# Attention kernel: the last head in two halves, own matmul orders for four of a head's eight pairs of steps, and the first phase's balances and copies issued at other places

## The chip, the cores and the metric

The kernel runs on one core of a Trainium2 chip. The metric is the device time of one execution in microseconds (us), as the median of several runs.

## The reference

Two attentions of 32 heads (head width 18, sequence 2048, width 576) are computed from the same `x` and mixed by a gate. In attention B all heads share one key and one value.

```python
def _A_ref(x, wqkv, wo):                       # 32 heads, each with its own k and v
    ...
    scores = jnp.einsum("bhqd,bhkd->bhqk", q, k) * scale
    p = _softmax(scores, axis=-1)
    o = jnp.einsum("bhqk,bhkd->bhqd", p, v)
    ...
def _B_ref(x, wq, wk, wv, wo):                 # k = x @ wk, v = x @ wv, shared
    ...
g = _sigmoid((x * gate_w).sum(-1, keepdims=True))
return g * a + (1 - g) * b
```

## The kernel before, in words

**First phase.** `project` multiplies the weights (14 column tiles, split into a high and a low float32r part) with `x` in 56 jobs of 14 matmuls each. `evict` rounds each result to two float16 parts on ScalarE and VectorE and writes them to DRAM. The factors `tv` that the evictions need come from `balance`: VectorE reduces the weights' sizes to `br` (line 201 or 206), TensorE turns it (209), VectorE forms `bd` (211 to 214), TensorE spreads it (219), VectorE makes `tv` (221 to 231). It is a generator; the tuple `at` names the matmuls of a job ahead of which it is continued. `shared_v` turns the shared values on TensorE and copies them to `vb` on VectorE (287), which frees a bank of PSUM.

**Second phase.** 64 heads `u`, 16 steps each; a step is one tile of 128 keys (and, 22 steps ahead, one tile of 128 queries for the maxima). The loop takes two steps at a time, A and B, so a head is eight pairs (T%16 = 0, 2, ... 14). A pair issues what a string lists, in that order, on TensorE:

- `sA0`..`sB3`: scores of 512 queries (line 551) into a bank of `ps` (four banks); ScalarE takes the exponential into `pt` (558).
- `mA0`..`mB3`: 512 scores of a head that comes 22 steps later (514) into a bank of `pm` (three banks); VectorE takes the row maximum into `mx` (523). `x` is a matmul with differences of keys; ScalarE puts its positive part into `xb` (517), and the `mA0` of the next pair is a VectorE operation that adds `xb` and takes the maximum (520, `junk`, followed by a read of its accumulator into `mx`). So `mA1` falls away, and a pair has seven such operations on VectorE and nine on ScalarE.
- `P`, or its halves `p` and `f`: step T-2's values times `pt`, summed in `acc` (564). `Q`, or `h` and `H`: the same for step T-1. A half has 256 columns, a whole one 512.
- `U`: a unit of the output projection (12 matmuls at line 678 and one sum on VectorE, or on ScalarE for heads 33 to 53).

Scores use the upper rows of the array and maxima the lower ones, so a score and a maximum that are neighbours in the string run side by side.

When a head's sum is complete (after `Q` of the pair T%16 = 0), `head_out` copies `acc` to `oe` on VectorE (574), and the next head's first product must wait for that. In the pair T%16 = 10, `max_rows` puts a reduction (529) and a transposition (531) on VectorE ahead of the pair's maxima.

The strings are `PLAIN` for most pairs, `END` for T%16 = 0, `AFTER` for T%16 = 2, and `UNIT`, `UNIT_END`, `UNIT2` where units of the output projection are due: in heads 33 to 53 in the pairs 0 and, every second head, 10; from step 944 on in every pair. From step 1002 there are no maxima left (`ALONE`).

**Tail.** After the last head, `last_out` copies `acc` (709, 710), turns it (713), scales it (717 to 719), turns it back (722), splits it (724, 725), sends it by DMA into `end` beside rows that `normalise(8)` has scaled (lines 602 to 621), and runs 32 units of three matmuls (735) and one sum on VectorE (738); each finished 128 rows of the output go out by DMA. `idle` issues matmuls whose results are not used.

Of the kernel before, what the change touches and what calls it, by code (L numbers as in the profile page):

```python
# [49 lines left out]
def gated_mix_kernel(ctx: ExitStack, tc: tile.TileContext, xT, wall, wv, wo, out):  # L50
# [277 lines left out]
    with tc.tile_pool(name="xs", bufs=6, side="right") as xsp:  # L328
# [215 lines left out]

    def step_scores(u, i, c, alone):
# [5 lines left out]
        nc.tensor.matmul(ps, kst(u)[b:b + 56, i * P:(i + 1) * P],  # L551
                         qs[u % 3][b:b + 56, c * 512:(c + 1) * 512], start=True, stop=True)
        PT["q"] = PT.get("q", []) + [(c, ps)]
        if alone and c == 0:
            return
        for c, ps in PT.pop("q"):
            pt = L["pt"].tile([P, 512], F32, name="pt")
            nc.scalar.activation(pt, ps, AF.Exp, scale=SCALE / LIFT ** 2)  # L558
            PT[u, i, c] = pt

    def step_pv(u, i, a, b):

        for j in range(4):
            nc.tensor.matmul(acc[32 * j:32 * j + 19, a:b], v_of(u, i), PT[u, i, j][:, a:b],  # L564
                             start=(i == 0 and a == 0), stop=(i == 15), skip_group_check=True)
        if b == 512:
            for j in range(4):
                del PT[u, i, j]

    OT = {}  # L570
# [19 lines left out]
    def normalise(t, at_end=False):  # L590
# [9 lines left out]
        yield  # L600
        yield
        nc.vector.reciprocal(sm[:n, :], sm[:n, :])
        (nc.vector if at_end else nc.gpsimd).tensor_tensor(sm[:n, :], sm[:n, :], gt[:n, :], op=OP.mult)
        yield
        dma(r_d[u0:u1, :].rearrange("h (s f) -> (h s) f", f=P), sm[:n, :])
        yield
        ot = OT.pop(t)
        R = L["work"].tile([P, S], F32, name="R", bufs=1)
        r0 = P * t
        while r0 < P * t + rows:  # L610
            u = r0 // DH
            n = min(DH * (u + 1), P * t + rows) - r0
            dma(R[r0 - P * t:r0 - P * t + n, :], r_d[u:u + 1, :].to_broadcast([n, S]))
            r0 += n
        yield
        if at_end:
            L["end"] = {y: L["pool"].tile([P, S], F32R, name=f"end{y}") for y in "hl"}
            for c in range(4):
                cs = slice(512 * c, 512 * c + 512)
                yield  # L620
                nc.vector.tensor_tensor(ot[:rows, cs], ot[:rows, cs], R[:rows, cs], op=OP.mult)
                split(ot[:rows, cs], L["end"]["h"][:rows, cs], L["end"]["l"][:rows, cs], nc.vector, nc.vector)
            return
# [74 lines left out]

    def last_out():

        oe, ot = (L["work"].tile([P, 512], F32, name=x, bufs=1) for x in ("oe", "oT"))
        oh, ol = (L["work"].tile([P, 512], F32R, name=x, bufs=1) for x in ("oh", "ol"))
        end = L["end"]

        def idle(n):
            for _ in range(n):
                nc.tensor.matmul(acc, qs[0][0:54, 0:P], qs[0][0:54, 0:512], start=True, stop=True)

        nc.scalar.activation(oe[:, 0:256], acc[:, 0:256], AF.Copy)
        nc.vector.tensor_copy(oe[:, 256:512], acc[:, 256:512])  # L710
        pt, pb = end_bank(), end_bank()
        for c in range(4):
            nc.tensor.transpose(pt[:, P * c:P * c + P], oe[:, P * c:P * c + P], ident)
        idle(5)
        r = L["work"].tile([P, 16], F32, name="rl")
        p4, o4 = (x.rearrange("p (c j d) -> p c j d", c=4, d=32) for x in (pt, ot))
        nc.vector.reciprocal(r.rearrange("p (j c) -> p c j", c=4), p4[:, :, :, DH])
        nc.vector.tensor_tensor(r, r, L["g"], op=OP.mult)
        nc.vector.tensor_tensor(o4, p4, r.rearrange("p (j c) -> p c j", c=4).unsqueeze(3).to_broadcast([P, 4, 4, 32]),
                                op=OP.mult)  # L720
        for c in range(4):
            nc.tensor.transpose(pb[:, P * c:P * c + P], ot[:, P * c:P * c + P], ident)
        idle(14)
        nc.scalar.activation(oh, pb, AF.Copy)
        nc.vector.tensor_tensor(ol, pb, oh.bitcast(F32), op=OP.subtract)
        r0 = DH * (NU - 1) - 8 * P
        for j in range(4):
            dma(end["h"][r0:P, 512 * j:512 * j + 512], oh[32 * j:32 * j + DH, :])
            dma(end["l"][r0:P, 512 * j:512 * j + 512], ol[32 * j:32 * j + DH, :], nc.scalar)
        w = WO[8]  # L730
        for st_ in range(16):
            for hf in range(2):
                fp = end_bank()
                for n, (a, b) in enumerate(PRODS):
                    nc.tensor.matmul(fp[:, 0:288], end[b][:, st_ * P:(st_ + 1) * P],
                                     w[a][:, 0, 288 * hf:288 * hf + 288], start=(n == 0), stop=(n == 2))
                dst = L["oacc"][:, st_, 288 * hf:288 * hf + 288]
                nc.vector.tensor_tensor(dst, fp[:, 0:288], dst, op=OP.add)  # L738
            dma(out[st_ * P:(st_ + 1) * P, :], L["oacc"][:, st_, :], nc.scalar if st_ % 2 else None)

# [14 lines left out]
    def when(T, f):  # L755
        at.setdefault(T, []).append(f)
# [46 lines left out]
    ALONE = "sA0 sA1 P U sA2 sA3 U sB0 sB1 h U sB2 sB3 H U"  # L803
    LEADS = "mA0 MA1 mA2 MA3 V.A mB0 MB1 mB2 MB3 V.B"
    order = None
    for T in range(-LEAD, NSTEP + 2, 2):
        if T == 0:
# [8 lines left out]
        order = LEADS if T < 0 else FIRST if T == 0 else ALONE if alone else (UNIT2 if T >= SEG[1][3] else UNIT_END if T % 16 == 0 else UNIT) if units else \  # L816
            END if T % 16 == 0 else AFTER if T % 16 == 2 and T > 2 else PLAIN
        for op in order.split():
# [12 lines left out]
            elif k == "s":  # L831
                if T < NSTEP:
                    step_scores(*divmod(T + second, 16), int(c), alone)
            elif k == "U":
                pull(min(units, 1))
                units -= min(units, 1)
            elif T >= 2:
# [13 lines left out]
    pull(10 ** 9)  # L851
    last_out()

# [33 lines left out]
```

## Time and profile before

| | |
|---|---|
| median of 3 runs | 2686.05 us (2685.97 to 2687.71) |
| profiled execution | 2688.33 us, its span 2686.0 us |
| TensorE busy | 2665.6 us (99%), 22697 matmuls |
| VectorE busy | 2428.2 us (90%) |
| ScalarE busy | 2402.0 us (89%) |
| first phase, until the first exponential | 277.2 us |
| second phase, until the last exponential ends | to 2659.0 us |
| tail | 27.0 us |

Rows of the profile give a start in us, a duration, engine, line, operation, `written<-read`, shapes and a count; `[0.17 <-PE pm L514]` says that the engine had been idle for 0.17 us and what ended that. "Busy" counts overlapping instructions once, so an engine that is busy all the time can still be waiting inside its instructions.

### The profile page before, as it was taken

Reading aid. Unit: us, or ns where it says so; the run is one execution under the profiler, and the core shown is the slowest. Engines: PE = TensorE matmul, PEld = TensorE weight load, DVE = VectorE, ACT = ScalarE, POOL = GpSimd, SP = SyncE. Lnnn points to the kernel's source line nnn. Section 1 sums busy time; section 2 is a strip of 40 time slices with the busy share of each in tenths; the row PEclk is TensorE's granted clock in tenths of the full one; section 3 lists DMA queues with packets and bytes.
Section 4 is the critical chain, followed back from the end, with each engine's and each line's share of the span. In section 5 each row is a group of like instructions: output and inputs, shape, how many; then the busy total and the mean of one; then the engine's idle time right before and its main releaser. Section 6 shows DMA issues by size and latency. Waiting matters only on the chain.

```text
span 2686.0 us, 59393 instructions
## 1 busy us (share of the span) xinstructions
PE 2665.6 (99%) x22697; PEld 905.2 (34%) x22697; DVE 2428.2 (90%) x4586; ACT 2402.0 (89%) x4810; POOL 278.8 (10%) x518
## 2 busy tenths in 40 slices
PE   9999999999999999999999999999999999999999
PEld 6778322222222222222222222322222232223444
DVE  7447999999999999999999999999999999998863
ACT  4341899999999999999999999999999999998875
POOL 4740000001001100100110002000200011011000
PEclk9999999999999999999999999999999999999999
DMA  6332000011001100210132112122121212122312
GB/s 201 124 112 78 21 20 20 19 37 40 28 17 46 44 20 18 54 32 20 36 76 82 43 51 85 42 56 58 57 67 50 56 52 61 39 71 85 89 36 94
DMA packets 126904, 150.19 MB, mean 56 GB/s; under 512 B 55272, under 2 KB 94344, under 8 KB 125421
## 3 DMA queue, kind: packets, MB, share of 16 engines
q1 hardware_dynamic: 112175, 119.08, 15.7%
q0 software_dynamic: 7968, 19.23, 2.1%
q10 hardware_dynamic: 6476, 8.08, 0.9%
q8 instruction: 178, 2.92, 0.5%
q14 instruction: 107, 0.88, 0.1%
HBM read 90.80 MB, written 46.45 MB: 51 GB/s over the span
## 4 chain that ended last, share of the span: by engine, by line
PE 84%; DVE 12%; issue 2%; DMA 1%; ACT 1%; SPq 0%; DVEq 0%; POOL 0%; ACTq 0%; POOLq 0%
PE acc L564 35%; PE ps L551 20%; PE pm L514 14%; DVE mx L523 7%; PE pm L678 4%; PE ps L514 3%; PE pm L248 3%; PE ps L248 2%; PE ps L297 2%; DVE junk L520 2%; DVE oe L574 1%; ACT pt L558 0%; SPq L56 0%; DVE oacc L738 0%; DVE norm_a L190 0%
## 5 line engine op out<-in xcount | busy, mean ns | idle before, releaser
L558 ACT ACTIVATE pt<-ps 128x512 f32<-128x512 f32 x4074 | 2109.1, 645 | 64.7 <-PE ps L551 47.0
L523 DVE TENSOR_REDUCE mx<-pm 128x1 f32<-128x512 f32 x3072 | 1918.4, 682 | 70.9 <-PE pm L514 34.5
L551 PE MATMUL ps<-qs,ksb 56*128 56x512 f16 x2688 | 810.5, 380 | 0.0
L514 PE MATMUL pm<-ksb,qs 54*128 54x512 f16 x2341 | 768.2, 381 | 1.9 <-DVE mx L523 0.6
L564 PE MATMUL acc<-pt,vb 128*19 128x512 f32 (+1 forms) x6392 | 598.5, 446 | 1.8
L564 PE MATMUL acc<-pt,vg 128*19 128x256 f32 (+1 forms) x5904 | 585.7, 468 | 1.2 <-DVE oe L574 0.5
L514 PEld LDWEIGHTS <-qs 54*128 54x128 f16 x4096 | 292.1, 94 | 598.0 <-issue 532.5
L551 PE MATMUL ps<-qs,ksa 56*128 56x512 f16 x1386 | 412.1, 380 | 0.7
L514 PE MATMUL pm<-ksa,qs 54*128 54x512 f16 x1232 | 401.4, 380 | 2.2 <-DVE mx L523 1.2
L520 DVE CUSTOM_DVE_ANT_0 junk<-pm,xb 128x512 bf16<-128x512 f32 x501 | 341.5, 682 | 11.1 <-PE pm L514 6.7
L551 PEld LDWEIGHTS <-ksb 56*128 56x128 f16 x2688 | 198.3, 93 | 402.5 <-issue 370.9
L517 ACT ACTIVATE xb<-ps 128x512 f32<-128x512 f32 x501 | 310.5, 620 | 7.7 <-PE ps L551 7.3
L564 PEld LDWEIGHTS acc<-pt,vb 128*19 128x19 f32 x6392 | 108.3, 96 | 248.1 <-issue 232.0
L533 POOL TENSOR_SCALAR mt<-mt 128x32 f32<-128x32 f32 x64 | 18.5, 290 | 1631.5 <-DVE mt L531 1631.5
L564 PEld LDWEIGHTS acc<-pt,vg 128*19 128x19 f32 x5904 | 100.7, 97 | 231.4 <-issue 223.9
L551 PEld LDWEIGHTS <-ksa 56*128 56x128 f16 x1408 | 100.3, 94 | 203.9 <-issue 186.7
L514 PE MATMUL ps<-kdb,qs 54*128 54x512 f16 x373 | 141.0, 378 | 0.1
L300 ACT ACTIVATE vst<-ps 128x288 f32<-128x288 f32 x32 | 13.2, 412 | 60.6 <-PE ps L297 60.6
L256 ACT ACTIVATE ph<-ps,tv 128x512 f16<-128x512 f32 x29 | 19.8, 685 | 50.8 <-PE ps L248 31.8
L256 ACT ACTIVATE ph<-pm,tv 128x512 f16<-128x512 f32 x27 | 18.3, 686 | 47.4 <-PE pm L248 30.8
L686 DVE TENSOR_TENSOR oacc<-pm,oacc 128x288 f32<-128x288 f32 x32 | 14.6, 458 | 49.1 <-PE pm L678 49.1
L262 DVE SCALAR_TENSOR_TENSOR pl<-pm,tv,ph 128x512 f16<-128x512 f32 x27 | 20.0, 748 | 37.6 <-ACT ph L256 28.5
(161 smaller groups left out, 1520.8 us busy)
## 6 DMA issues: line engine op xcount, KB each, us to landing
qs<-qkh SPq DMA_DIRECT2D x244, 72.0 KB
qs<-qkl SPq DMA_DIRECT2D x122, 72.0 KB
onh<-oh SPq DMA_DIRECT2D x32, 256.0 KB
onl<-ol SPq DMA_DIRECT2D x32, 256.0 KB
oih<-onh SPq DMA_DIRECT2D x16, 512.0 KB
oil<-onl SPq DMA_DIRECT2D x16, 512.0 KB
ot<-oe SPq DMA_DIRECT2D x220, 36.0 KB
R<-r_d SPq DMA_DIRECT2D x55, 144.0 KB
```

The source lines that it names most:

```text
L248: nc.tensor.matmul(fp[:, a0:b0], w[a][:kr, k, :], X[b][:kr, k, s0 + a0:s0 + b0], start=(n == 0), stop=(n == len(PROJ) - 1), skip_group_che ...
L256: nc.scalar.activation(h, fp, AF.Copy, scale=t)
L297: nc.tensor.matmul(fp[:, 0:288], X[b][:kr, k, st_ * P:(st_ + 1) * P], w[a][:kr, k, :], start=(n == 0), stop=(n == len(PROJ) - 1))
L514: nc.tensor.matmul(pm, qs[u % 3][b:b + 54, i * P:(i + 1) * P], k, start=True, stop=True)
L517: nc.scalar.activation(MX["x", u, i], pm, AF.Relu)
L520: nc.vector.tensor_tensor_reduce(junk, pm, MX.pop(("x", u, i)), 1.0, -3e38, op0=OP.add, op1=OP.max, accum_out=MX[u][:, i, c:c + 1])
L523: nc.vector.tensor_reduce(MX[u][:, i, c:c + 1], pm, axis=AX.X, op=OP.max)
L551: nc.tensor.matmul(ps, kst(u)[b:b + 56, i * P:(i + 1) * P], qs[u % 3][b:b + 56, c * 512:(c + 1) * 512], start=True, stop=True)
L558: nc.scalar.activation(pt, ps, AF.Exp, scale=SCALE / LIFT ** 2)
L564: nc.tensor.matmul(acc[32 * j:32 * j + 19, a:b], v_of(u, i), PT[u, i, j][:, a:b], start=(i == 0 and a == 0), stop=(i == 15), skip_group_ch ...
L574: nc.vector.tensor_copy(oe, acc)
L678: nc.tensor.matmul(fp[:, 0:288], o[b][:r, t, s2 * P:(s2 + 1) * P], w[a][:r, t, 288 * hf:288 * hf + 288], start=(n == 0), stop=(n == 3 * nt ...
```

## The change

Three edits.

1. First phase: `balance(0)` and `balance(2)` are continued at later matmuls, `shared_v(0)` stands ahead of `flush()`, and the weights `W[3]` are prepared ahead of job 9 rather than ahead of job 6.
2. Second phase: new strings for T%16 = 0 and 2, and strings of their own for 8 and 10 (until now `PLAIN`):

```diff
-        project(3, hold=True, gen=bal, at=(12,))
-        project(4, hold=True, gen=bal, at=(9,))
+        project(3, hold=True)
+        project(4, hold=True, gen=bal, at=(3, 10))
...
+        shared_v(0)
         flush()
-        WP.append(prep_w(W[3]))
-        shared_v(0)
         for n in range(6, 12):
...
+            if n == 9:
+                WP.append(prep_w(W[3]))
...
-            project(n, gen=bal, at={15: (7,), 16: (4,)}.get(n, ()))
+            project(n, gen=bal, at={16: (2, 11)}.get(n, ()))
...
-    END = "mA0 sA0 mB0 p mA2 sA1 x mB2 sA2 sA3 mA3 f sB0 mB1 mB3 sB1 sB2 Q sB3"
-    AFTER = "mB3 sA0 mB1 mB2 sA1 p sA2 x sA3 mB0 f mA0 sB0 mA3 sB1 h mA2 sB2 H sB3"
+    END = "mB2 sA0 mB3 mB1 sA1 p sA2 mA2 sA3 mA0 sB0 f x mB0 sB1 mA3 sB2 Q sB3"
+    AFTER = "mB1 mA3 sA0 sA1 sA2 mA0 P sA3 mA2 sB0 mB2 x sB1 mB0 h sB2 mB3 H sB3"
+    BEFORE_ROWS = "mA0 sA0 mB3 sA1 mB1 sA2 p sA3 mA2 f sB0 mB2 sB1 mB0 x sB2 mA3 Q sB3"
+    ROWS = "mB3 sA0 mA3 sA1 mB1 sA2 P mB2 sA3 sB0 mA0 x sB1 mB0 h sB2 mA2 H sB3"
...
-            END if T % 16 == 0 else AFTER if T % 16 == 2 and T > 2 else PLAIN
+            {0: END, 2: AFTER if T > 2 else PLAIN, 8: BEFORE_ROWS, 10: ROWS}.get(T % 16, PLAIN)
```

3. The last head and the tail: the last head's steps take 1024 queries against two key tiles each, first one half of the queries, then the other. `last_pv` sums a half in 256 columns of `acc`; `last_half(0)` turns, scales, splits and sends the first half while the second half's scores run; `normalise(8)` is issued at fixed pairs, its broadcast `R` in two halves; `last_units` holds the 32 units of the output, of which two are issued in the last pair, three around `last_half(1)`, and 27 behind it. Four of them (5, 8, 11, 14) are copied out by ScalarE and added by GpSimd. The matmuls of `idle` are gone.

```diff
+    LAST = "sA0 sA1 c P U sA2 sA3 U sB0 sB1 h U c sB2 sB3 u H U u"
+    TL = 16 * (NU - 1)
...
+    LAST_U = (TL + 14,)
...
+    TAIL = {TL: [N8], TL + 2: [N8], TL + 6: [N8, N8, N8], TL + 8: [HALF[0]], TL + 10: [N8]}
...
-    last_out()
+    next(HALF[1])
+    for n in (1, 2, 30):
+        for _ in range(n):
+            next(END_U, None)
+        next(HALF[1], None)
```

How the program's rows move. First VectorE around the end of a head, before; `mx` rows with a count are maxima, `junk` and the `mx` row under it are one `mA0`, `oe` is the head's copy:

```order
L520 ISA junk,mx_1891<-pm,xb 128x512
L520 ISA mx_1891 128x1
L520 ISA junk,mx_1891<-pm,xb 128x512
L520 ISA mx_1891 128x1
L523 TENSOR_REDUCE mx_1891<-pm 128x1 x6
L574 COPY oe<-acc 128x512
L523 TENSOR_REDUCE mx_1891<-pm 128x1 x4
L520 ISA junk,mx_1891<-pm,xb 128x512
L520 ISA mx_1891 128x1
L523 TENSOR_REDUCE mx_1891<-pm 128x1 x8
```

and now:

```order
L521 ISA junk,mx_1891<-pm,xb 128x512
L521 ISA mx_1891 128x1
L524 TENSOR_REDUCE mx_1891<-pm 128x1 x4
L521 ISA junk,mx_1891<-pm,xb 128x512
L521 ISA mx_1891 128x1
L524 TENSOR_REDUCE mx_1891<-pm 128x1 x2
L588 COPY oe<-acc 128x512
L524 TENSOR_REDUCE mx_1891<-pm 128x1 x2
L521 ISA junk,mx_1891<-pm,xb 128x512
L521 ISA mx_1891 128x1
L524 TENSOR_REDUCE mx_1891<-pm 128x1 x10
```

The two `mA0` that stood directly behind each other ahead of the copy are apart now, and the copy stands behind two maxima of the pair's last part.

Second, VectorE from the pair 6 to the pair 10 of the same head, before (`m` and `mt` are the rows of `max_rows`):

```order
L523 TENSOR_REDUCE mx_1891<-pm 128x1 x6
L520 ISA junk,mx_1891<-pm,xb 128x512
L520 ISA mx_1891 128x1
L523 TENSOR_REDUCE mx_1891<-pm 128x1 x6
L520 ISA junk,mx_1891<-pm,xb 128x512
L520 ISA mx_1891 128x1
L529 TENSOR_REDUCE m_1900<-mx_1891 128x16
L531 STREAM_TRANSPOSE mt<-m_1900 128x32
L523 TENSOR_REDUCE mx_1892<-pm 128x1 x6
```

and now:

```order
L524 TENSOR_REDUCE mx_1891<-pm 128x1 x6
L521 ISA junk,mx_1891<-pm,xb 128x512
L521 ISA mx_1891 128x1
L521 ISA junk,mx_1891<-pm,xb 128x512
L521 ISA mx_1891 128x1
L524 TENSOR_REDUCE mx_1891<-pm 128x1 x6
L530 TENSOR_REDUCE m_1900<-mx_1891 128x16
L532 STREAM_TRANSPOSE mt<-m_1900 128x32
L524 TENSOR_REDUCE mx_1892<-pm 128x1 x4
```

Here it is the other way round: the pair 8 begins with `mA0`, directly behind the one that ends the pair 6, and the rows of `max_rows` now follow six maxima.

Third, TensorE behind the last head's scores, before (`qs` feeds the last of the 14 matmuls of `idle`, `endh` and `endl` are the rows to be projected, `woh` and `wol` the weights):

```order
L707 LDWEIGHTS qs_92
L707 MATMUL acc<-qs_92 128x512
L735 MATMUL ps<-woh,endh 128x288
L735 MATMUL ps<-woh,endl 128x288
L735 MATMUL ps<-wol,endh 128x288
L735 MATMUL pm<-woh,endh 128x288
L735 MATMUL pm<-woh,endl 128x288
```

and now:

```order
L764 MATMUL pm<-woh,endh_39802 128x288
L764 MATMUL pm<-woh,endl_39803 128x288
L764 MATMUL pm<-wol,endh_39802 128x288
L578 MATMUL acc<-pt,vg 19x256 x4
L764 MATMUL pm<-woh,endh_39802 128x288
L764 MATMUL pm<-woh,endl_39803 128x288
L764 MATMUL pm<-wol,endh_39802 128x288
L578 MATMUL acc<-pt,vg 19x256 x16
L764 MATMUL ps<-woh,endh_39802 128x288
L764 MATMUL ps<-woh,endl_39803 128x288
L764 MATMUL ps<-wol,endh_39802 128x288
L735 MATMUL pm<-ident,oe 128x128 x2
```

Two units stand ahead of the last products with `pt`, and a third ahead of the transposition of `oe`; they read the first half's tiles.

More of the change, by code (lines that the diff above doesn't have):

```diff
@@ L568, in step_pv, with last_pv @@
                 del PT[u, i, j]
+    def last_pv(n, tiles):
+        u = NU - 1
+        half, n = divmod(n, 8)
+        for i in (2 * n + e for e in tiles):
+            for j in range(4):
+                nc.tensor.matmul(acc[32 * j:32 * j + 19, 0:256], v_of(u, i),
+                                 PT[u, i, 2 * half + j // 2][:, 256 * (j % 2):256 * (j % 2) + 256],
+                                 start=(i == 0), stop=(i == 15), skip_group_check=True)
+            for c in range(2):
+                del PT[u, i, 2 * half + c]
     OT = {}
@@ L687, in out_proj @@
                     yield
+    END_T = []
     def prep_last():
+        for h in range(2):
+            END_T.append({y: L["pool"].tile([P, S // 2], F32R, name=f"end{y}{h}") for y in "hl"})
+        L["rl"] = L["pool"].tile([P, 16], F32, name="rl")
         L["g"] = L["pool"].tile([P, 16], F32, name="gl")
@@ new lines, in last_half @@
+    def last_half(h):
+        if not h:
+            L["last"] = [L["work"].tile([P, 512], F32R if x[1] in "hl" else F32, name=x, bufs=1)
+                         for x in ("oe", "oT", "oh", "ol")]
+        oe, ot, oh, ol = (x[:, 256 * h:256 * h + 256] for x in L["last"])
+        if h:
+            nc.scalar.activation(oe[:, 0:P], acc[:, 0:P], AF.Copy)
+            nc.vector.tensor_copy(oe[:, P:256], acc[:, P:256])
+        else:
+            nc.vector.tensor_copy(oe, acc[:, 0:256])
+        yield
+        pt = ps_m.tile([P, 512], F32, name="pm")[:, 0:256]
+        for c in range(2):
+            nc.tensor.transpose(pt[:, P * c:P * c + P], oe[:, P * c:P * c + P], ident)
+        r = L["rl"][:, 8 * h:8 * h + 8]
+        rc = r.rearrange("p (j c) -> p c j", c=2)
+        p4, o4 = (x.rearrange("p (c j d) -> p c j d", c=2, d=32) for x in (pt, ot))
+        nc.vector.reciprocal(rc, p4[:, :, :, DH])
+        nc.vector.tensor_tensor(r, r, L["g"][:, 8 * h:8 * h + 8], op=OP.mult)
+        nc.vector.tensor_tensor(o4, p4, rc.unsqueeze(3).to_broadcast([P, 2, 4, 32]), op=OP.mult)
+        yield
+        pb = ps_m.tile([P, 512], F32, name="pm")[:, 0:256]
+        for c in range(2):
@@ L730, in last_out @@
-        w = WO[8]
[L731 to L737, printed above, removed]
+            for y, o, e in (("h", oh, nc.sync), ("l", ol, nc.scalar if h else nc.gpsimd)):
+                dma(END_T[h][y][r0:P, 256 * j:256 * j + 256], o[32 * j:32 * j + DH, :], e)
@@ new lines, in end_bank, with last_units @@
+    def end_bank(n=[0]):
+        n[0] += 1
+        return ps_s.tile([P, 512], F32, name="ps") if n[0] % 7 < 4 else ps_m.tile([P, 512], F32, name="pm")
+    def last_units():
+        w = WO[8]
+        for n in range(32):
+            st_, hf = divmod(n, 2)
+            end = END_T[st_ // 8]
+            fp = end_bank() if n > 1 else ps_m.tile([P, 512], F32, name="pm")
+            for m, (a, b) in enumerate(PRODS):
+                nc.tensor.matmul(fp[:, 0:288], end[b][:, (st_ % 8) * P:(st_ % 8 + 1) * P],
+                                 w[a][:, 0, 288 * hf:288 * hf + 288], start=(m == 0), stop=(m == 2))
+            dst = L["oacc"][:, st_, 288 * hf:288 * hf + 288]
+            if 4 <= n < 16 and n % 3 == 2:
+                part = L["work"].tile([P, 288], F32, name="part", bufs=2)
+                nc.scalar.activation(part, fp[:, 0:288], AF.Copy)
+                nc.gpsimd.tensor_tensor(dst, part, dst, op=OP.add)
+            else:
@@ L841, in gated_mix_kernel @@
         pull(units)
+        for f in TAIL.get(T, ()):
+            next(f, None)
         if slow and M % 16:
```

86 lines of the change are left out of this document (42 added, 44 removed).

## The prediction

> **What bounds the kernel now.** I read the page first, then timelines of a plain head (head 20), the waits of the first phase, and the timeline of the tail. The page calls every engine busy, so the timeline decides. ScalarE, between two `xb` of neighbouring pairs:
>
> ```profile
> 1015.20 0.65 ACT L517 ACTIVATE xb<-ps 128x512 f32<-128x512 f32 x1
> 1015.68 4.09 ACT L558 ACTIVATE pt<-ps 128x512 f32<-128x512 f32 x8
> 1019.61 0.65 ACT L517 ACTIVATE xb<-ps 128x512 f32<-128x512 f32 x1
> ```
>
> Nine operations take 4.41 us, 0.49 each, with no gap. So ScalarE cannot do a head (72 operations) in under 35.28 us. VectorE and TensorE where a head begins (I name a pair by T%16; pair 0 runs from the score at 994.29, pair 2 from 999.02 to 1003.54), and the next head's copy:
>
> ```profile
> 994.09 0.68 DVE L520 CUSTOM_DVE_ANT_0 junk<-pm,xb 128x512 bf16<-128x512 f32 x1
> 994.29 0.39 PE L551 MATMUL ps<-qs,ksb 56*128 56x512 f16 x1
> ...
> 994.95 0.69 DVE L520 CUSTOM_DVE_ANT_0 junk<-pm,xb 128x512 bf16<-128x512 f32 x1 [0.17 <-PE pm L514]
> ...
> 995.56 3.67 DVE L523 TENSOR_REDUCE mx<-pm 128x1 f32<-128x512 f32 x6
> ...
> 996.30 0.37 PE L514 MATMUL pm<-ksb,qs 54*128 54x512 f16 x1
> ...
> 998.04 1.05 PE L564 MATMUL acc<-pt,vb 128*19 128x512 f32 x8
> 999.02 0.39 PE L551 MATMUL ps<-qs,ksb 56*128 56x512 f16 x1
> ...
> 999.16 0.69 DVE L574 COPY oe<-acc 128x512 f32<-128x512 f32 x1
> 999.25 0.38 PE L551 MATMUL ps<-qs,ksb 56*128 56x512 f16 x1
> ...
> 999.77 2.47 DVE L523 TENSOR_REDUCE mx<-pm 128x1 f32<-128x512 f32 x4
> ...
> 1002.66 0.39 PE L551 MATMUL ps<-qs,ksb 56*128 56x512 f16 x1
> ...
> 1003.54 0.39 PE L551 MATMUL ps<-qs,ksb 56*128 56x512 f16 x1
> ```
> ```profile
> 1034.92 0.69 DVE L574 COPY oe<-acc 128x512 f32<-128x512 f32 x1
> ```
>
> From copy to copy a head takes 35.76 us: 0.48 above ScalarE's floor, and no order of matmuls can gain more per plain head. Pair 0 takes 4.73, pair 2 4.52. In them VectorE runs without a pause at 0.60 us an operation (six from 995.56 to 999.16), so it is VectorE that sets them, with fourteen operations and the copy; ScalarE would need 8.82 for both.
>
> **The second phase, step by step.** Two `mA0` in a row cost extra: the second begins 0.86 us after the first (994.09, 994.95), where an operation otherwise takes 0.60. That is 0.26 us of VectorE, and it holds TensorE: the matmul at 996.30 is the fourth on three banks and starts 0.74 after the maximum that began at 995.56 (its 0.68 and a signal). The new `END` begins with `mB2`, so this goes. I redo pairs 0 and 2 by hand in the new order, with t from the first score of pair 0. VectorE is free at 0.40, since the `mA0` of the pair before began at -0.20. The reader at another engine starts 0.43 us after its matmul does:
>
> ```profile
> 994.72 1.72 ACT L558 ACTIVATE pt<-ps 128x512 f32<-128x512 f32 x3
> ```
>
> VectorE then starts mB2 at 0.42, the next three at 1.02, 1.62 and 2.22, mA0 at 2.82, mB0 and mA3 at 3.44 and 4.04, and copies at 4.64. No maximum has to wait long for its bank: the fourth is due at 1.41 and its bank is free at 1.16 (0.42 + 0.74). So TensorE reaches `Q` at 3.46 and the next pair at 4.45 (now 4.73). In pair 2 VectorE goes on at 5.25. `P` must wait for the copy until 5.38, but three scores stand ahead of it, so it is due at 5.42 only, and those scores keep ScalarE fed. The last maximum ahead of `h` is held for 0.13, and pair 4 begins at 8.92, where it now begins at 9.25 (1003.54 less 994.29). Gain 0.33. ScalarE's 8.82 allows it. But VectorE's next start is now 0.13 later than it is after a plain pair, and that holds the third maximum of the following pair: I take back 0.08 of the 0.13 and keep 0.25. Bounds: nothing gained, and 0.43 (9.25 less 8.82).
>
> TensorE's own need does not change. Every string, old and new, has nine slots of matmuls and two products' worth of `acc`. `AFTER` trades two halves for one whole product and has one slot more without a partner. The rows for that:
>
> ```profile
> 1012.27 0.39 PE L551 MATMUL ps<-qs,ksb 56*128 56x512 f16 x1
> ...
> 1012.96 0.37 PE L551 MATMUL ps<-qs,ksb 56*128 56x512 f16 x1
> ...
> 1014.25 0.39 PE L514 MATMUL pm<-ksb,qs 54*128 54x512 f16 x1
> ...
> 1016.68 0.39 PE L551 MATMUL ps<-qs,ksb 56*128 56x512 f16 x1
> ...
> 1021.30 0.39 PE L551 MATMUL ps<-qs,ksb 56*128 56x512 f16 x1
> ```
>
> A whole product takes 1.29 from slot to slot (1012.96, 1014.25), a half 0.88 (1002.66, 1003.54), a slot 0.23 (999.02, 999.25): 1.06 plus the slot against 1.30, nothing either way. The Trainium skill (TensorEngine Tiling (Array Packing), Key Properties) says that a change of tiling mode drains the array; by that alone `AFTER`, with one change fewer, would gain. The rows bear out the price of a change, but the slot eats it.
>
> Pairs 8 and 10: now 4.41 and 4.62 (1012.27, 1016.68, 1021.30). VectorE's rows there:
>
> ```profile
> 1016.48 0.68 DVE L520 CUSTOM_DVE_ANT_0 junk<-pm,xb 128x512 bf16<-128x512 f32 x1
> ...
> 1017.66 3.63 DVE L523 TENSOR_REDUCE mx<-pm 128x1 f32<-128x512 f32 x6
> ```
>
> `max_rows` adds 0.58 (1.18 less 0.60). `BEFORE_ROWS` begins with `mA0` directly behind the one that ends the pair before, so the 0.26 appears here. Redone like pair 0: VectorE starts at 0.66, 1.26, 1.86, 2.46, 3.06, 3.66, 4.26; `mA3` is held by its bank until 3.20, so `Q` and the next pair come at 4.49 (now 4.41). With `max_rows` behind it, `ROWS` starts VectorE at 5.45 and is held before `h`: 9.12 for both, now 9.03. That is a loss of 0.09, between a gain of 0.10 (ScalarE's 8.82 and half of what is left) and a loss of 0.35 (all of the 0.26 on top of the 0.09). I stay at 0.09, since the same hand working gives today's pairs to 0.03.
>
> Counts: pairs 0 and 2 both change in 37 heads (1 to 32, 54 to 58). In heads 33 to 53 a unit stands ahead of `AFTER` and TensorE is the limit of those two pairs:
>
> ```profile
> 1725.80:1736.40 10.60, 10.60 (x94) 3.69 (x93) 9.42 (x20) 9.81 (x20) 0.00 (x0) 1.00 0.26 79
> ```
>
> TensorE is busy throughout, VectorE (third) 9.42 and ScalarE (fourth) 9.81 of 10.60, so I cost `AFTER` there at nothing (0.1 either way). Pairs 8 and 10 change in 59 heads. Sum: 37 x -0.25 + 59 x 0.09 = -9.2 + 5.3 = -3.9 us.
>
> **First phase.** TensorE's waits:
>
> ```profile
> PE acc L209 <- DVE br L206: 1.3, 1, 1.3
> ...
> PE ps L248 <- DVE vb L287: 1.2, 1, 1.2
> PE acc L209 <- DVE br L201: 1.0, 1, 1.0
> ```
> ```profile
> 66.01 1.41 DVE L206 TENSOR_REDUCE br<-norm_a 128x1 f32<-128x576 f32 x2
> 67.33 0.74 DVE L262 SCALAR_TENSOR_TENSOR pl<-ps,tv,ph 128x512 f16<-128x512 f32 x1
> ...
> 69.27 0.57 DVE L141 TENSOR_TENSOR wl<-wst,wh 64x128 fp32r<-64x128 f32 x2
> ```
>
> The first turn of `br` moves five matmuls later, about 0.23 each (as a slot): 1.2 us against a wait of 1.0. `vb` is copied ahead of evictions it stood behind: 1.2. The second turn moves nine matmuls, 2.1 us against 1.3; but TensorE is then 2.2 us earlier (1.0 + 1.2) and VectorE, by my estimate, only 1.3 (the 1.0 and what waited for ScalarE's work on `W[3]`), so some 0.2 stays; and a second `pl` and `wl` (0.74 + 0.57) now stand ahead of `bx`, for which the spread at matmul 11 waits about 0.5. Together 1.0 + 1.2 + 1.3 - 0.7 = 2.8 us. What is late next is the eviction of job 16, whose bank is asked for again only three jobs later. `W[3]` is needed at job 12, three jobs after its new place. Bounds: a gain of 1 and, with all three waits gone, of 3.5.
>
> **Tail.**
>
> ```profile
> 2657.46 1.52 ACT L558 ACTIVATE pt<-ps 128x512 f32<-128x512 f32 x2
> ...
> 2664.83 3.95 ACTq L56 DMA_DIRECT2D endl<-ol  x4
> ```
> ```profile
> 2646.40 0.69 DVE L621 TENSOR_TENSOR ot<-ot,R 110x512 f32<-110x512 f32 x1 [6.01 <-DMA R<-r_d]
> ...
> 2648.20 0.69 DVE L621 TENSOR_TENSOR ot<-ot,R 110x512 f32<-110x512 f32 x1
> ...
> 2664.11 0.69 DVE L725 TENSOR_TENSOR ol<-ps,oh 128x512 fp32r<-128x512 f32 x1 [1.44 <-ACT oh L724]
> 2668.14 0.46 DVE L738 TENSOR_TENSOR oacc<-ps,oacc 128x288 f32<-128x288 f32 x1 [3.34 <-PE ps L735]
> ...
> 2680.99 1.25 DVE L738 TENSOR_TENSOR oacc<-pm,oacc 128x288 f32<-128x288 f32 x3
> ```
> ```profile
> 2664.00:2667.50 3.50, 2.94 (x14) 1.21 (x13) 0.69 (x1) 0.07 (x1) 0.00 (x0) 1.00 0.17 42
> 2667.50:2671.00 3.50, 3.50 (x15) 3.50 (x16) 1.83 (x4) 0.00 (x0) 0.00 (x0) 0.51 0.40 125
> ```
>
> Now the last exponential ends at 2658.98, the first unit's sum begins 9.2 us later, the 32 sums end 14.1 later (2682.24; 0.41 each at full clock), and 3.7 remain for the last output: 27.0. The chain of copies and turns has operations half as wide, so I estimate 4.2 us until `ol` is split (now 5.8, 2664.80). By then five units are issued; the eleven left of the first half cover the landing of the second (about 3.3 now, 2664.80 to 2668.14). ScalarE issues four transfers (3.95) ahead of the sum's copy of unit 5, and its bank is needed by unit 12: TensorE waits until about 8.4, four units bring 10.0, sixteen at 0.41 bring 16.6, and 3.7 remain: 20.3. Gain 6.7, between 5 (two units' worth later) and 9 (without the wait for unit 5's bank). Against it, `R` lands at 2646.4; three scalings of 1.8 each (2646.40, 2648.20), two of which can start with the first half of `R`, now stand on VectorE ahead of the first half's copy of `acc`, due near 2646, and the next product waits for that copy. I take 1.0 (0 to 2.5). The clock was at half in one stretch (0.51), in which VectorE made 4 sums where 8 fit, which is 1.5 us; I assume that once more and, the `idle` matmuls being gone, most of a second time: 1.2 more. Sum: 6.7 - 1.0 - 1.2 = 4.5 us.
>
> **Sum.** -3.9 - 2.8 - 4.5 = -11.2. The profiled execution took 2688.33 (span 2686.0); the runs' median is 2686.05, so I subtract from the median: 2674.8, written 2675.
>
> **Rivals.**
> - The orders gain all that ScalarE allows: no stall is left, 0.42 in 37 heads and 0.10 in 21: -17.6 - 7.3, 2661. For it: ScalarE has no gap of its own. Against: VectorE's 0.26 moved into pair 8. 15%.
> - The orders of pairs 0 and 2 gain nothing, since VectorE's 0.13 and the copy come back as stalls in pair 4: 59 x 0.09 - 7.3 = -2, 2684. 16%.
> - Slower: VectorE stays behind all round the head. The `mA0` pair's 0.26 comes on top of the 0.09 instead of beside it, pair 0 starts late and gains nothing: 59 x 0.35 - 7.3 = +13.4, 2699. It decides from 0.22 a head, where it eats tail and first phase and 0.2%. Against it: plain pairs leave VectorE 0.15 each. 7%.
> - The clock: the 0.51 follows a window in which TensorE was 84% busy (2.94 of 3.50). Without `idle` it may fall for two windows more than now, 1.5 each: 1.8 above the forecast, and `last_half(1)` itself at half clock about 1 more: 2678. The Trainium skill (TensorE: Matmul & The Clock Gate, Part 1) gives free-running windows of 3.4 us and a half clock after an idle one; the half window agrees in length, but none before it was idle. 12%.
> - That the change does less than it says: with only five units early the tail gains 3 less, 2678; it is in the forecast's range.
>
> **How the numbers follow.** The forecast with its bounds (2668 to 2681) has 50%. The range takes in the first rival nearly and the second: 2661 to 2684. A measurement of this kernel can tell about 0.2% (5.4 us) from no change: faster 0.77 (forecast, clock, first rival), same 0.15, slower 0.08.
>
> **What would show it.** Right: two `junk` 0.86 apart no longer ahead of the copy `oe` but at the start of pair 8; pairs 0 and 2 near 9.0 together, pairs 8 and 10 near 9.1; a plain head near 35.6; no wait of TensorE for `vb` and about 0.7 left of those for `br` and `bd`; the first exponential near 274.4; about 21 to 22 us from the last exponential to the end. Wrong: the length of a head unchanged or longer, pairs 8 and 10 above 9.3, or a tail above 24.

## The result, and the profile after

The changed kernel takes 2669.97 us (median of 4 runs, 2669.63 to 2671.51); the kernel before took 2686.01 in the runs beside it. The ratio is 0.9940, 95% interval 0.9927 to 0.9952: 16.0 us less, where 11 were forecast. Both profiled executions are slower than their medians (2688.33 before; 2671.51 now, span 2669.7), so the stages below tell where the time went, and the medians how much it is. The stages against the forecast, from the rows below and those of before:

| stretch | forecast | measured |
|---|---|---|
| start to the first exponential | -2.8 | 277.22 to 276.29: -0.9 |
| first exponential to the end of the last one | -3.9 + 1.0 | 2381.8 to 2370.0: -11.8 |
| from there to the end | -6.7 + 1.2 | 27.0 to 23.4: -3.6 |

So the time lies in the forecast's range, but all three terms were off: two gains came out smaller than forecast and the third about four times as large, and in the sum they partly cancel.

The first and the last row are those of one execution. Six of the experiments below have the same first phase: in five of them the first exponential starts at 275.31 to 275.60, in the sixth at 277.07; without the change it starts at 277.22 and, in `orders_only`, at 277.28. So most executions gain 1.6 to 2.0 there. Seven experiments have the same tail: it takes 22.5 to 22.8 in five of them, 23.1 and 23.7 in the other two, so most gain 4.2 to 4.5.

ScalarE's first and last exponentials, after:

```profile
276.29 4.03 ACT L560 ACTIVATE pt<-ps 128x512 f32<-128x512 f32 x8 [0.40 <-PE pm L515]
...
2644.47 1.79 ACT L560 ACTIVATE pt<-ps 128x512 f32<-128x512 f32 x3
```

Head 20 in the timeline after. The scores shown are the last of a pair, which stand at the same place in old and new strings: the pair before this head, pairs 0, 2, 6, 8 and 10.

```profile
987.92 0.39 PE L553 MATMUL ps<-qs,ksb 56*128 56x512 f16 x1
...
992.39 0.39 PE L553 MATMUL ps<-qs,ksb 56*128 56x512 f16 x1
992.59 0.68 DVE L588 COPY oe<-acc 128x512 f32<-128x512 f32 x1
...
996.86 0.39 PE L553 MATMUL ps<-qs,ksb 56*128 56x512 f16 x1
...
1005.41 0.68 DVE L521 CUSTOM_DVE_ANT_0 junk<-pm,xb 128x512 bf16<-128x512 f32 x1
1005.61 0.39 PE L553 MATMUL ps<-qs,ksb 56*128 56x512 f16 x1
1006.27 0.69 DVE L521 CUSTOM_DVE_ANT_0 junk<-pm,xb 128x512 bf16<-128x512 f32 x1 [0.17 <-PE pm L515]
...
1010.11 0.39 PE L553 MATMUL ps<-qs,ksb 56*128 56x512 f16 x1
...
1014.70 0.39 PE L553 MATMUL ps<-qs,ksb 56*128 56x512 f16 x1
```

Pairs 0 and 2 take 8.94 (before 9.25), pairs 8 and 10 take 9.09 (before 9.03), and the two `junk` 0.86 apart stand at the start of pair 8, as foretold. A plain head takes 35.53 instead of 35.76.

Worked out from the starts of all exponentials, the stretch between the first and the last splits so: pairs 0 and 2 of the 37 plain heads -11.5; pairs 0 to 6 of heads 33 to 53 -3.5; pairs 8 and 10 of heads 1 to 58 +2.7; the last head +0.8; the rest -0.3.

The first phase, TensorE's waits after:

```profile
PE acc L219 <- DVE bd L214: 1.5, 1, 1.5
PE ps L248 <- ACT xh L339: 0.7, 1, 0.7
```

The three waits are gone, but a new one of 1.5 us has come. The timeline shows its cause, and a table of stretches what followed (the column behind the busy times is the granted clock):

```profile
67.79 1.55 DVE L214 TENSOR_SCALAR bd<-ident,bx 2x2 f32<-2x2 f32 x1
68.04 1.27 POOL L139 TENSOR_TENSOR wl<-wst,wh 128x512 fp32r<-128x512 f32 x1
```
```profile
66.50:70.00 3.50, 1.99 (x9) 1.36 (x9) 2.89 (x7) 0.00 (x0) 2.79 (x4) 1.00 0.33 112
...
71.00:72.00 1.00, 1.00 (x4) 0.80 (x3) 0.61 (x3) 0.15 (x1) 0.00 (x0) 0.55 0.06 16
72.00:73.00 1.00, 1.00 (x3) 0.72 (x3) 0.43 (x1) 1.00 (x2) 0.17 (x1) 0.50 0.00 0
73.00:74.00 1.00, 1.00 (x4) 0.81 (x3) 0.98 (x2) 0.12 (x1) 0.76 (x2) 0.50 0.08 29
74.00:75.00 1.00, 1.00 (x5) 0.83 (x4) 0.00 (x0) 0.00 (x0) 1.00 (x3) 0.75 0.61 209
```

`bd` is four numbers; on VectorE it took 0.22 before and now 1.55, and it ended at 69.34, where GpSimd's `wl` ended at 69.31. TensorE stood idle for 1.5 us until 69.39, and from 71.1 to 74.5 the clock was at half.

The tail after, VectorE, ScalarE, GpSimd and the transfer queues, and a stretch of it (the last two columns are the share of 16 DMA engines and GB/s):

```profile
2631.33 0.69 DVE L637 TENSOR_TENSOR ot<-ot,R 110x512 f32<-110x512 f32 x1
...
2633.12 0.42 DVE L731 COPY oe<-acc 128x256 f32<-128x256 f32 x1
...
2650.81 0.42 DVE L128 TENSOR_TENSOR ol<-pm,oh 128x256 fp32r<-128x256 f32 x1 [0.28 <-ACT oh L124]
...
2651.27 3.66 ACTq L56 DMA_DIRECT2D endl<-ol  x4
...
2654.97 0.41 ACT L769 ACTIVATE part<-pm 128x288 f32<-128x288 f32 x1 [4.19 <-DVE oacc L772]
...
2655.43 0.40 PE L764 MATMUL pm<-woh,endh 128*128 128x288 f32 x1 [1.08 <-ACT part L769]
...
2659.04 0.40 PE L764 MATMUL pm<-woh,endh 128*128 128x288 f32 x1 [0.54 <-ACT part L769]
...
2662.94 1.26 DVE L772 TENSOR_TENSOR oacc<-ps,oacc 128x288 f32<-128x288 f32 x3
```
```profile
2659.00:2667.00 8.00, 4.67 (x33) 4.43 (x33) 4.45 (x11) 0.00 (x0) 0.81 (x1) 1.00 1.02 387
```

The first half's copy waits behind the third scaling, as forecast; TensorE waits for the first `part`, as forecast; but the last sum ends at 2664.20 and the kernel 5.5 us later, not 3.7, with the DMA engines full.

### The profile page after: what moved, and what is told of

Same layout as the page of the kernel before. It is cut to its first block, busy times and chain, and to the rows that moved or that the text cites. A ratio compares the mean times of both kernels' runs of the same rounds, so it can differ in the third digit from the quotient of the medians.

```text
span 2669.7 us, 58607 instructions
## 1 busy us (share of the span) xinstructions
PE 2652.4 (99%) x22278; PEld 898.0 (34%) x22278; DVE 2421.4 (91%) x4588; ACT 2393.3 (90%) x4814; POOL 283.8 (11%) x526
## 3 DMA queue, kind: packets, MB, share of 16 engines
q1 hardware_dynamic: 112593, 119.38, 15.7%
## 4 chain that ended last, share of the span: by engine, by line
PE 93%; DVE 5%; ACT 1%; DMA 1%; issue 1%; SPq 0%; ACTq 0%; DVEq 0%
PE acc L566 38%; PE ps L553 26%; PE pm L515 13%; PE pm L695 4%; PE ps L515 4%; PE ps L248 3%; PE pm L248 3%; DVE mx L524 2%; PE ps L297 2%; DVE junk L521 0%; ACT pt L560 0%; DVE norm_a L190 0%; DVE pl L262 0%; DMA R<-r_d 0%; DVE oacc L772 0%
## 5 line engine op out<-in xcount | busy, mean ns | idle before, releaser
L566 PE MATMUL acc<-pt,vb 128*19 128x256 f32 (+1 forms) x6144 | 592.4, 457 | 0.0
L566 PE MATMUL acc<-pt,vg 128*19 128x256 f32 (+1 forms) x5496 | 561.7, 480 | 0.3
L518 ACT ACTIVATE xb<-ps 128x512 f32<-128x512 f32 x501 | 319.6, 638 | 7.7 <-PE ps L553 7.3
L566 PEld LDWEIGHTS acc<-pt,vg 128*19 128x19 f32 x5496 | 93.2, 97 | 213.1 <-issue 209.7
```

Of the source, the lines that this page charges most:

```text
L518: nc.scalar.activation(MX["x", u, i], pm, AF.Relu)
```

## The experiments

Each is one edit to the changed kernel unless said otherwise; times are medians of four runs, to be compared with 2670.0, and ratios are against the kernel before, run beside it. Single traces differ by stretches of 3.4 us at half clock that come in some executions and not in others: near 71, as above, and near 280, at the start of head 0, which costs 1.1 us (head 0 takes 36.39 in the profile after and 35.31 in `orders_only`). So traces are compared stage by stage.

**The four strings alone, in the kernel before.**

```diff
 # before, with only these four of the change
 END, AFTER, BEFORE_ROWS, ROWS
```

> The kernel before with the four new strings alone; first phase and last head as before. The two traces put 11.6 us of the gain between the first exponential and the start of the last head's last one, and the last head itself lost 0.8 of that. Theory (the four orders alone make that gain, and the stages add up): 12.4 us less than before, 2673.6, with a plain head at 35.53 (before 35.76) and heads 33 to 53 at 37.79 (before 37.93). Rival (what the first phase hands over, or the new last head, helps the heads): about what the prediction gave the orders, 4 us less, 2682.

2674.75 us, ratio 0.9957 (0.9942 to 0.9972): 11.3 less than before. A plain head takes 35.54; heads 33 to 53, from exponential to exponential, take 37.76 on average (37.89 before, 37.76 in the changed kernel). That is near the theory's 12.4 and far from 4: the rival falls, and the strings make their gain by themselves.

**`bd` on ScalarE.**

```diff
-        nc.vector.tensor_scalar(dg, ident[0:2, 0:2], x, None, op0=OP.mult)
+        if g:
+            nc.scalar.activation(dg, ident[0:2, 0:2], AF.Copy, scale=x)
+        else:
+            nc.vector.tensor_scalar(dg, ident[0:2, 0:2], x, None, op0=OP.mult)
```

> The changed kernel with the second balance's bd computed on ScalarE instead of VectorE, nothing else. Theory (VectorE's bd, 1.55 us instead of 0.22, was held until GpSimd's wl ended; TensorE waited 1.5 us for it, and the granted clock fell to half from about 71.4 to 74.4 because of that wait, another 1.5 us): bd takes 0.2 to 0.3 us, TensorE's wait for it goes, the clock stays at 1.00 there, the first exponential starts about 3 us earlier (273.3 instead of 276.3) and the kernel takes 2667. Rival 1 (the clock's fall has another cause): only 1.5 us is won, first exponential near 274.8. Rival 2 (TensorE is early and waits for the next thing, the evictions that need tv): under 0.5 us won.

2668.33 us, ratio 0.9933 (0.9917 to 0.9950). Its timeline and stretches:

```profile
68.08 0.29 ACT L215 ACTIVATE bd<-ident,bx 2x2 f32<-2x2 f32 x1 [4.38 <-DVE bx L212]
68.26 1.29 POOL L139 TENSOR_TENSOR wl<-wst,wh 128x512 fp32r<-128x512 f32 x1
...
273.76 2.55 ACT L563 ACTIVATE pt<-ps 128x512 f32<-128x512 f32 x5 [0.40 <-PE pm L518]
```
```profile
66.50:70.00 3.50, 3.19 (x14) 2.29 (x14) 2.36 (x11) 0.29 (x1) 2.89 (x4) 1.00 0.33 112
...
72.00:73.00 1.00, 1.00 (x6) 0.82 (x5) 1.00 (x2) 0.15 (x1) 0.76 (x2) 1.00 0.02 8
```

The clock stays at 1.00, and the first exponential comes 2.5 us earlier than in the profile after (276.29 to 273.76). That seems near the theory's 3, but the median moved by 1.6 only, and the other traces say why. `tail_two`, an experiment further down, has the first phase of the changed kernel:

```profile
68.39 1.54 DVE L214 TENSOR_SCALAR bd<-ident,bx 2x2 f32<-2x2 f32 x1
...
275.33 4.03 ACT L560 ACTIVATE pt<-ps 128x512 f32<-128x512 f32 x8 [0.40 <-PE pm L515]
```
```profile
66.50:70.00 3.50, 2.00 (x10) 1.29 (x8) 3.32 (x7) 0.00 (x0) 2.87 (x4) 1.00 0.33 112
...
72.00:73.00 1.00, 1.00 (x6) 0.78 (x5) 0.24 (x2) 0.55 (x1) 0.00 (x0) 1.00 0.00 0
```

There `bd` is held as long and TensorE is as little busy, but the clock stays at 1.00. So it does in five of the seven traces in which `bd` is held; it falls in two, the profile after and `after_q_whole`. From the turn of `br` (line 209) to the first exponential it is 208.0 us with `bd` on ScalarE, 209.2 in the five, and 210.8 in the two. The hold therefore costs 1.2 us each time, and the half clock 1.6 more where it comes, so in most executions the gain is near rival 1's 1.5. What decides whether the clock falls is not shown: in the four traces without the hold it did not fall here, but four are few beside two of seven.

**The preparation of `W[5]` behind job 16; `bd` stays on VectorE.**

```diff
-            if c == 0 and mt + 1 < MT:
+            if c == 0 and mt + 1 < MT and n != 16:
                 WP.append(prep_w(W[mt + 1]))
             project(n, gen=bal, at={16: (2, 11)}.get(n, ()))
+            if n == 16:
+                WP.append(prep_w(W[mt + 1]))
```

> The changed kernel with the preparation of W[5] (its wl on GpSimd, 1.27 us, and a small wl on VectorE) issued behind the matmuls of job 16 instead of ahead of them; bd stays on VectorE. Theory (bd was held by the GpSimd operation that ran beside it): bd takes 0.22 us again, TensorE's wait for it is under 0.4 us, the clock stays at 1.00 from 70 to 76, and the first exponential starts near 273.8, as with bd on ScalarE; the kernel near 2668. Rival (bd is slow by itself at this place, or through GpSimd's issue of transfers): bd still takes over 1 us and the first exponential starts near 276.3.

2668.55 us, ratio 0.9939 (0.9923 to 0.9956):

```profile
67.85 0.29 DVE L214 TENSOR_SCALAR bd<-ident,bx 2x2 f32<-2x2 f32 x1
...
273.87 2.55 ACT L562 ACTIVATE pt<-ps 128x512 f32<-128x512 f32 x5 [0.40 <-PE pm L517]
```

With no GpSimd operation beside it, `bd` is short on VectorE too, and the first exponential comes as early as with `bd` on ScalarE. (The edit moves two small `wl` of VectorE, 0.28 each, behind `bd` as well.) So it was `wl` that held `bd`: in all seven traces with the hold, `bd` ends 0.03 to 0.04 us behind `wl`. The Trainium skill (SBUF — State Buffer, Who interferes with whom) says that VectorE and GpSimd share a pair of ports under an exclusive lock, which VectorE takes in two-port modes (`tensor_scalar` can enter one) or with two inputs in SBUF, and that the one that comes second is blocked for the other's whole instruction. The ends 0.03 apart and both experiments agree with the blocking; that `wl` came first does not show, since the profile has `bd` begin 0.25 ahead of it.

**`PLAIN` again in pairs 8 and 10.**

```diff
-            {0: END, 2: AFTER if T > 2 else PLAIN, 8: BEFORE_ROWS, 10: ROWS}.get(T % 16, PLAIN)
+            {0: END, 2: AFTER if T > 2 else PLAIN}.get(T % 16, PLAIN)
```

> The changed kernel with the old string PLAIN back in pairs 8 and 10 of a head, nothing else. Theory (the new strings of pairs 8 and 10 cost 0.055 us a head, 9.085 instead of 9.03, and help nothing beside it): 59 heads x 0.055 = 3 us less, 2666.7, pair 8 at 4.41 and pair 10 at 4.62 again. Rival (with the new END and AFTER, VectorE comes to pair 8 later than before, and PLAIN there would lose more than the new strings do): 0 to 5 us more than the changed kernel, 2670 to 2675.

2667.38 us, ratio 0.9931 (0.9916 to 0.9946). Pairs 8 and 10 are at 4.41 and 4.62 again, and heads 1 to 58 take 2.5 us less in all. The two new strings were a loss of 0.05 a head, and helped nothing else.

**The first two maxima of pair 8 exchanged.**

```diff
-    BEFORE_ROWS = "mA0 sA0 mB3 sA1 ..."
+    BEFORE_ROWS = "mB3 sA0 mA0 sA1 ..."
```

> The changed kernel with the first two maxima of the string for pair 8 exchanged, so that mA0 no longer follows the mA0 that ends the pair before; nothing else. Theory (the 0.26 us that two junk in a row cost VectorE is what makes pair 8 4.50 instead of 4.41): pair 8 at 4.41 to 4.42 and pair 10 at 4.58 or less: 59 x 0.08 = 5 us less, 2665; 9.0 for both pairs. Rival (the place of max_rows and the halves of products set these pairs, and the 0.26 is covered): pairs 8 and 10 at 9.08, time 2670.

2661.17 us, ratio 0.9909 (0.9894 to 0.9923): the largest step of all. VectorE, and the last scores of pairs 6, 8 and 10:

```profile
1000.72 0.68 DVE L521 CUSTOM_DVE_ANT_0 junk<-pm,xb 128x512 bf16<-128x512 f32 x1
1001.33 0.08 DVE L521 DVE_READ_ACCUMULATOR2_ANT mx<- 128x1 f32 x1
1001.39 0.69 DVE L524 TENSOR_REDUCE mx<-pm 128x1 f32<-128x512 f32 x1
1001.99 0.68 DVE L521 CUSTOM_DVE_ANT_0 junk<-pm,xb 128x512 bf16<-128x512 f32 x1
```
```profile
1000.93 0.39 PE L553 MATMUL ps<-qs,ksb 56*128 56x512 f16 x1
...
1005.38 0.39 PE L553 MATMUL ps<-qs,ksb 56*128 56x512 f16 x1
...
1009.84 0.39 PE L553 MATMUL ps<-qs,ksb 56*128 56x512 f16 x1
```

Pairs 8 and 10 take 8.91, where ScalarE needs 8.82; the theory had 9.0. Pair 8 gave 0.05 (4.50 to 4.45) and pair 10 gave 0.13 (4.59 to 4.46). From the `junk` that ends pair 6, VectorE's third operation starts 1.88 later instead of 2.08, so the pairs got 0.18 of those 0.20.

**Two buffers for `junk`.**

```diff
-            junk = lead.tile([P, 512], BF16, name="junk", bufs=1)
+            junk = lead.tile([P, 512], BF16, name="junk", bufs=2)
```

> The changed kernel with two buffers for the tile junk instead of one, nothing else. Theory A (the second junk in a row starts 0.86 us after the first because it writes the tile that the first wrote): 0.60 between them, pair 8 near 4.41 and pairs 8 and 10 at 9.0 instead of 9.085: 59 x 0.085 = 5 us less, 2665. Theory B (it is the operation's own: its result is read out by a second instruction, READ_ACCUMULATOR, and the next such operation waits for that): still 0.86, time 2670.

2666.20 us, ratio 0.9925 (0.9910 to 0.9939); pairs 8 and 10 at 9.00, 4.3 us less in heads 1 to 58. VectorE at the start of pair 8:

```profile
1001.98 0.68 DVE L521 CUSTOM_DVE_ANT_0 junk<-pm,xb 128x512 bf16<-128x512 f32 x1
1002.58 0.09 DVE L521 DVE_READ_ACCUMULATOR2_ANT mx<- 128x1 f32 x1
1002.75 0.69 DVE L521 CUSTOM_DVE_ANT_0 junk<-pm,xb 128x512 bf16<-128x512 f32 x1
```

0.77 between the two: 0.09 of the 0.26 came from the one buffer, and the pairs got just that. 0.17 remain: the second `junk` starts 0.17 behind the first one's readout, where a maximum mostly starts together with it or up to 0.06 later. That fits theory B, and each theory was right in part.

**`P` of `AFTER` in two halves, heads 33 to 53 only.**

```diff
-    "mB1 mA3 sA0 sA1 sA2 mA0 P sA3 mA2 sB0 mB2 x sB1 mB0 h sB2 mB3 H sB3"
+    "mB1 mA3 sA0 sA1 sA2 mA0 p sA3 mA2 f sB0 mB2 x sB1 mB0 h sB2 mB3 H sB3"
```

> The changed kernel with the whole product P of AFTER made into two halves, one slot apart, in heads 33 to 53 alone. Theory (in those heads TensorE sets pairs 0 and 2, and each separate turn to the products costs it about 0.24 us; the old AFTER had four such turns and the new one three, which is their gain of 0.255): the gain goes, pair 2 there takes 6.81 instead of 6.57 from last score to last score, 21 x 0.24 = 5 us more, 2675. Rival (the places of the maxima made the gain, and TensorE has room): pair 2 stays at 6.57 and the time at 2670.

2672.98 us, ratio 0.9951 (0.9936 to 0.9966). The last score but one of pair 0 and the last of pair 2 of head 40, in the changed kernel and then in this one:

```profile
1719.85 0.38 PE L553 MATMUL ps<-qs,ksb 56*128 56x512 f16 x1
...
1726.42 0.39 PE L553 MATMUL ps<-qs,ksb 56*128 56x512 f16 x1
```
```profile
1720.04 0.38 PE L553 MATMUL ps<-qs,ksb 56*128 56x512 f16 x1
...
1726.85 0.39 PE L553 MATMUL ps<-qs,ksb 56*128 56x512 f16 x1
```

6.57 against 6.81 (6.82 with the old string), so one more turn to the products costs this pair 0.24. Pair 4 gives 0.05 back; the heads take 3.5 us more. The theory's mechanism stands, at two thirds of its size.

**`h` and `H` of `AFTER` made whole, heads 33 to 53 only.**

```diff
-    "... x sB1 mB0 h sB2 mB3 H sB3"
+    "... x sB1 mB0 sB2 mB3 Q sB3"
```

> The changed kernel with the two halves h and H of AFTER made into one whole product Q behind sB2 mB3, in heads 33 to 53 alone: one turn to the products fewer than the changed kernel, where the split P had one more. Theory (a turn costs TensorE 0.24 us and TensorE still sets that pair): pair 2 of these heads 6.33 instead of 6.57, up to 21 x 0.24 = 5 us less, but pair 4 may give some back as it did in the last experiment (0.07): 2665 to 2667. Rival (ScalarE, with nine operations of 0.49 in pair 2, is the next limit, since pair 2 by the starts of the exponentials is 4.55 and cannot go under 4.41): at most 0.14 a head, 3 us less, or, where the later lower half makes the exponentials wait, slower.

2675.00 us, ratio 0.9958 (0.9944 to 0.9973). Pair 2, between the same two scores, became longer, 6.65, and pair 4 shorter by 0.05; heads 33 to 53 take 37.78 on average instead of 37.76. The theory falls here: one turn fewer gains nothing more, which the rival allowed for. What sets these pairs now was not settled. The rest of the loss lies mostly in the last head, where that string is not used: in the profiled execution `sm` landed later there, and so did `R`:

```profile
2621.84 0.95 DVE L617 RECIPROCAL sm<-sm 96x128 f32<-96x128 f32 x1 [4.63 <-DMA sm<-sum_d]
...
2629.43 0.69 DVE L637 TENSOR_TENSOR ot<-ot,R 110x512 f32<-110x512 f32 x1 [2.06 <-DMA R<-r_d]
```

The first half's copy came later with it, TensorE waited 2.2 us for that copy instead of 0.8, and the clock was at half from 2634.0 to 2640.8; the last head took 3.7 us more. Why the load was late was not tried.

**Two edits of the last head.**

```diff
-    for y, o, e in (("h", oh, nc.sync), ("l", ol, nc.scalar if h else nc.gpsimd)):
+    for y, o, e in (("h", oh, nc.sync), ("l", ol, nc.gpsimd)):
...
-    TL + 6: [N8, N8, N8], TL + 8: [HALF[0]]
+    TL + 6: [N8, N8], TL + 8: [HALF[0], N8]
```

> The changed kernel with two edits in the last head: the first half's copy oe stands ahead of the third scaling instead of behind it, and the second half's ol leaves by GpSimd's queue instead of ScalarE's. Theory: the copy starts 0.7 to 0.8 earlier and the pair with 0.50 us of idle ScalarE shrinks from 4.62 to near 3.9 (0.7 us); ScalarE makes the first part about 3 us earlier, TensorE's waits of 1.08 and 0.54 for it go, the outputs start 1 to 1.6 us earlier, and the end, which the queue of outputs sets (5.5 us from the last sum to the end), moves by the same: 2 us less in all, 2668, and 21.8 us from the last exponential's end to the end instead of 23.4. Rival (the outputs' transfers, 16 engines busy from 2659 on, set the end whatever TensorE does): 0.7 us less, 2669.3.

2667.48 us, ratio 0.9930 (0.9914 to 0.9947). The last head is 0.6 shorter and the tail takes 21.6 instead of 23.4 from the last exponential. Its last exponentials, the first `part`, and a stretch near the end:

```profile
2642.23 1.80 ACT L560 ACTIVATE pt<-ps 128x512 f32<-128x512 f32 x3
...
2648.51 0.41 ACT L769 ACTIVATE part<-pm 128x288 f32<-128x288 f32 x1
```
```profile
2656.00:2663.00 7.00, 3.25 (x25) 3.01 (x23) 3.75 (x10) 0.00 (x0) 0.00 (x0) 0.99 1.03 387
```

The last sum ends 2.2 us earlier counted from the last exponential (15.7 instead of 17.9), but the end only 1.9, and 0.9 to 1.3 against the 22.5 to 22.8 of most traces: the outputs' transfers are full at 387 GB/s here too, and they set the end.

**All four that gained** (`bd` on ScalarE, the exchange, the two edits of the last head), alone and with two buffers for `junk`.

> The changed kernel with four edits that the runs so far have shown to gain: bd of the second balance on ScalarE, the first two maxima of pair 8's string exchanged, the first half's copy ahead of the third scaling, and the second half's ol by GpSimd's queue. If the stages add up: 8.8 (exchange) + 2.5 (last head) + 1.6 to 2.5 (first phase) less than the changed kernel's 2670.0: 2656 to 2657. If they do not (the next stage takes back what is won): between 2657 and 2661, the exchange alone.

> The same four edits and two buffers for junk. Theory (two buffers helped only where two junk stood in a row, and the exchange leaves none): the same time as the four edits alone, within 1 us, pairs 8 and 10 at 8.91. Rival (the single buffer held VectorE elsewhere too): up to 2 us less.

2657.00 us (2656.16 to 2657.81), ratio 0.9894 (0.9879 to 0.9908), and 2656.73 with the second buffer, ratio 0.9892 (0.9878 to 0.9907). The gains add up: 13.0 us less than the changed kernel, 29 less than before. The second buffer gains nothing once no two `junk` stand in a row, so that was all it did.

## Why the prediction was right, and where not

- **The sum.** Forecast 11.2, measured 16.0. The middle was 8.9 too low (-2.9 against -11.8), start and tail together 3.8 too high in the profiled execution. That the time came out well inside the range owes something to luck, since errors of opposite sign partly cancel.
- **Pairs 0 and 2, plain heads.** 11.5 us instead of 9.2. The hand working gave 8.92 and the trace 8.94; the 0.08 that was taken back for pair 4 was not due. VectorE's rows bear the mechanism out (two `mA0` no longer ahead of the copy): from the `mA0` ahead of pair 0 to the first maximum of pair 4 it takes 9.67 instead of 9.90, without another pause in either trace. That is 0.23 of the 0.31; the rest, in which the whole `P` of `AFTER` can have a part here too, was not tried alone.
- **Pairs 8 and 10.** 0.05 a head instead of 0.09, and the count of 59 was too high for pair 10: in 11 of those heads it holds a unit. The step was right in sign and cause: the exchange parts the two `junk`, and pairs 8 and 10 fall to 8.91.
- **Heads 33 to 53 "at nothing": the step that failed.** "One slot more without a partner" was supposed to eat what the whole product saves. These heads gained 3.5 us instead. Split in two again, that product costs 0.24 more, as much as the old string lost. The Trainium skill's rule (TensorEngine Tiling (Array Packing), Key Properties), that a change of tiling mode drains the array, would have given a gain here, of a size that the page does not state; the prediction cited it and set it aside. Its reach is limited too: the next turn saved, `h` and `H` made whole, gained nothing.
- **First phase: 0.9 in the profiled execution and 1.6 to 2.0 in most, instead of 2.8.** The three waits went as foretold. "What is late next is the eviction of job 16" named the wrong thing: it was `bd`, held by GpSimd's `wl`, which in the old places ran 1.7 us later than `bd`. The hold cost 1.2, and 1.6 more where a half clock followed. The prediction had counted only VectorE's own rows ahead of `bx`, and no other engine's.
- **Tail: 3.6 in the profiled execution and 4.2 to 4.5 in most, instead of 5.5.** `ol` was split at 5.0 us after the last exponential, not 4.2, and TensorE's wait for the first `part`, behind the four transfers as named, ended at 9.2 (2655.43), not 8.4; a second one of 0.54 was not foreseen. The 3.7 from the last sum to the end was taken over from before, but it is a queue of transfers, and now it took 5.5 (4.6 to 5.8 in the other traces with this tail, whose last sums end at the same place within 0.3). By my estimate, 1.8 us at 387 GB/s are 2.4 outputs of 288 KB more that had not left when the last sum ended. In the profiled execution the transfers ran at only 229 GB/s from 11 to 13 us after the last exponential, where the other traces with this tail have 358 to 386; why is not known. The clock did not fall there (1.00 in all stretches of the last 20 us with work), so the 1.2 for that was not due.
- **The rivals.** None came about. The orders gained far more than forecast, which is the direction of the first rival, but pairs 8 and 10 kept their stall; that they need not is what the exchange showed. (The first rival's 0.42 a head follows from no row: ScalarE's floor allows 0.48.)

## What to carry to other kernels

When an instruction is moved, look at what runs beside its new place on *every* engine, not only at what stands ahead of it on its own: four numbers on VectorE cost 1.2 us because a GpSimd operation ran there. Costs of neighbourhood (two accumulating operations in a row, one more turn between kinds of matmuls) are small, 0.2 us each, but a loop over 59 heads pays them every time, and the order that avoids them costs nothing. A stretch that is copied from the old trace as a constant, like the time from the last sum to the end, has its own limit, and it must be asked whether the change leaves that limit alone. And two single traces can differ by something that comes only in some executions: the 2.5 us between two profiles here were 1.2 in most.

## What was not expected of the hardware

- A VectorE operation on four numbers took 1.55 us instead of 0.22 beside a GpSimd operation of 1.27.
- The share of busy time did not decide the clock: it fell to half behind 1.99 us of work in 3.50 (the profile after) and stayed at 1.00 behind 2.00 in 3.50 (`tail_two`).
- An operation that reads out an accumulator is followed by another such one after 0.86 us (0.77 with a second buffer for its output), and by an ordinary maximum mostly after 0.61 to 0.66.
